# Moving one load four steps later, reshaping the warm-up and scaling rows a step sooner in a fused retention and feed-forward kernel

## The chip, the cores and the metric

The kernel runs on one core of a Trainium2 chip. The metric is device time in microseconds (us): the time of one execution, the median of the runs shown. The engines are named as in the profile: PE is TensorE's matmul stream and PEld its weight loads, DVE is VectorE, ACT is ScalarE, POOL is GpSimd, and SP is the engine whose queue issues nearly all the DMA transfers here. Each engine runs its own instructions strictly in the order in which they were built, and engines wait for one another only where one needs what another has made, or a buffer that another still uses.

## The reference

Per batch and head, scores between queries and keys are decayed by position and multiplied into the values; the result goes through a two-layer feed-forward block with the activation h - tanh(h).

```
ret = (scale * q @ k.T * Dmat) @ v        # 8 batches, 8 heads, 576 positions, 64 per head
x = ret laid out as (4608 tokens, 512)
h = x @ w_in                              # 512 -> 2048
out = (h - tanh(h)) @ w_out               # 2048 -> 512
```

## The kernel before, in words

The 576 positions are cut into 9 column chunks of 64, numbered c or n from 0 to 8; a chunk of all 8 batches gives 512 tokens. Within a chunk the retention part works on (chunk, batch) pairs numbered j = 8 c + b, as products inside the chunk plus a running state that carries what came before. The feed-forward part of chunk n runs over 16 slices f of the 2048 hidden values: `mm1(n, f)` makes a hidden slice (12 matmuls), `mm2(n, f)` multiplies it with a slice of w_out into four output banks o0 to o3 (12 matmuls). To keep precision each fp32 operand is split into two words, a high and a low one (names ending in h and l), and three products of words are added.

The work is staged in three parts.

1. **Seq part** (lines 583 to 629, `k` from 0 to 31): `mm1` of chunks 0 and 1, while the weights arrive and are split. Each weight slice passes through a chain over ACT and DVE (`guard` at lines 96 and 99, `unit` at lines 106 to 118, `finish` at line 125) that is advanced by `step()`. The hidden slices of chunks 0 and 1 are copied out of PSUM by ACT (lines 391 and 397) and spilled to DRAM, because w_out is not there yet. Retention work of chunks 0 and 1 is put in by `entry`. The keys of chunk 0 that build its states stand in two tiles, `krows[0]` and `krows[1]`; ACT multiplies each by a table (`scale_k`, line 576, four instructions each). `krows[1]` is loaded at k = 3 and scaled at k = 7, and first used at k = 8.
2. **Late part** (lines 630 to 642, 32 steps): `mm2` of chunk 1, steps 0 to 15, then of chunk 0, steps 16 to 31. Spilled slices are fetched back into three buffers (`fetch`, line 421, tiles named s), get their tanh and subtraction (`resume`, lines 426 and 427) and are split into words (`words`, lines 433 and 434). At step k the code issues, in this order: `words` of slice k + 1, `resume` of slice k + 2, `fetch` of slice k + 4, and the matmuls of slice k. At step 15 `mm2` closes chunk 1: its four banks are copied out by ACT and DVE (lines 468 and 470) and stored, and step 16 starts chunk 0 in the same banks.
3. **Main part** (lines 644 to 655): `mm1` and `mm2` of chunks 2 to 8 in turn, with retention of the next chunk put in between.

In the late and main parts retention is put in by `entry3(j)`, which computes the outputs of pairs j and j + 1 (and of j + 2, if b > 0), and at its end loads what the next one needs: the value rows (`vr`, `load_part(then, 1)`), a single column (`one`, `load_one`) and the queries and keys after that (`qk`, `load_part(.., 0)`). The first two parts of this data are needed early in the next `entry3`, the `qk` near its end, where it gives the next scores. `load_part(j, 0)` also loads the table of a new chunk (`qtab`, line 162), which stands in a single buffer. POOL multiplies each loaded tile by its table (`prep`, line 207). In the late part `entry3(16)`, `entry3(18)` and `entry3(21)` stand ahead of steps 3, 13 and 20.

All loads and stores of these parts are issued by SP, in order. An SP instruction that must wait (for a landed transfer or a buffer to come free) holds back all those behind it.

At the very start the PE runs warm-up matmuls on zeros (`busy`, line 498): 26 of 128 columns and 8 of 256 columns, ahead of the first scores, which wait for their data.

Of the kernel before, what the change touches and what calls it, by code (L numbers as in the profile page):

```python
# [19 lines left out]
P = 128  # L20
NF = DF // P
NCC = DM // P
C = 64
# [6 lines left out]


STEP = float(np.arctanh(0.5) / (1.06 * 2.0**-15))
WARM = 26

NI = NC * B

# [23 lines left out]
def behind(tc, name):  # L60

    tc.add_manual_dep(
        tc.nc.cur_bb.bb.instructions[-1], name,
        mybir.DependencyInfo(mybir.DependencyClass.Sync, mybir.DependencyReason.DATA), reason="paced",
    )
# [3 lines left out]
def retention_ffn(ctx: ExitStack, tc: tile.TileContext, ins, out, spill):  # L69
# [86 lines left out]
    def load_qtab(c):  # L156
        if c not in qtabs:
            if c == 1:
                qtabs[c] = const.tile([P, 4, C], F32, tag="wo6", name="qtab1")
            else:  # L160
                qtabs[c] = pool.tile([P, 4, C], F32, tag="qtab", bufs=1, name=f"qtab{c}")
            nc.sync.dma_start(qtabs[c], qtab_d[c - 1])

    def load_part(j, t):

        if j >= NI:
            return
        c, b = divmod(j, B)
        if t == 0:
            load_qtab(c)  # L170
        early = c == 1 and b // 2
        if early and early > 1:

            part = const.tile([P, 2, 2, 4, C], F32, tag=f"wo{2 * (early - 2) + t}", name=f"early{j}_{t}")
        elif early and t == 1:
            part = pool.tile([P, 2, 2, 4, C], F32, tag="one", bufs=1, name=f"vr{j}")
        else:
            part = pool.tile([P, 2, 2, 4, C], F32, tag=("qk", "vr")[t], bufs=2 - t, name=f"{('qk', 'vr')[t]}{j}")
        nc.sync.dma_start(part, qkv_d[c - 1, b : b + 2, :, 2 * t : 2 * t + 2].rearrange("u p t i s -> p u t i s"))
        if early and early > 1:  # L180
            behind(tc, pace[-1])
        parts[j, t] = part
        for u in range(2):
            loaded.setdefault(j + u, Parts([None, None])).parts[t] = part[:, u]
# [12 lines left out]
    def prep(j, t, n=2):  # L197

        if j >= NI:
            return  # L200
        c = j // B
        a = parts[j, t][:, :, 0]
        if t == 0:
            table = qtabs[c].unsqueeze(1).broadcast_to([P, n, 4, C])
        else:
            table = vtab[:, c].unsqueeze(1).unsqueeze(3).broadcast_to([P, n, 4, D])
        nc.gpsimd.tensor_tensor(a, a, table, op=ALU.mult)  # L207
# [16 lines left out]
    def m_score(j, sc):  # L224
        a = loaded[j]
        return [
            (sc[half(c), i], a[half(c), 1, i, :], a[half(c), 0, i, :], True, True) for i in range(4) for c in range(2)
        ]
# [23 lines left out]
    def run(same, other):  # L252

        while same or other:
            for ms in (same, other):
                for out_, w, x, start, stop in ms[:2]:
                    nc.tensor.matmul(out_, w, x, start=start, stop=stop)  # L257
                del ms[:2]

    def after_score(j, sc, n):  # L260

        if j < B:

            pm = pool.tile([P, 2, 4, C], F32, tag="gh", name=f"pm{j}")
            nc.vector.tensor_tensor(pm[:, 0], sc[:, 0], decay, op=ALU.mult)
        else:

            pm = parts[j, 0][:, :, 1]
            nc.vector.tensor_tensor(
                pm, sc, mask.unsqueeze(1).unsqueeze(1).broadcast_to([P, n, 4, C]), op=ALU.mult,  # L270
            )
        for u in range(n):
            scored[j + u] = pm[:, u]
# [20 lines left out]
    def bank(name, tag):  # L294
        return psp.tile([P, 2, 4, D], F32, tag=tag, bufs=2 if tag == "h" else 1, name=name)
# [5 lines left out]
    def pair(what, j, bank):  # L301
        return what(j, bank[:, 0]) + what(j + 1, bank[:, 1])
# [10 lines left out]
            more[1]()  # L313
        add_state(j, new)

    def entry3(j):


        c0, b = divmod(j, B)
        single, states = b > 0, c0 < NC - 1  # L320
        then = j + 2 + single
        o = bank(f"own{j}", "own")
        outs, scores = pair(m_out, j, o), []
        if single:
            two = bank(f"two{j + 2}", "new")
            run(m_score(j + 2, two[:, 1]), outs[:8])
            after_score(j + 2, two[:, 1:], 1)
            outs = outs[8:]
            if states:

                new = bank(f"new{j + 2}", "h")
                run(m_state(j + 2, new[:, 0]), outs[:8])
                outs = outs[8:]
                kept = pool.tile([P, 1, 4, D], F32, tag="cv", bufs=4, name=f"kept{j + 2}")
                nc.scalar.copy(kept, new[:, :1])
        if states:
            new = bank(f"new{j}", "h")
            run(pair(m_state, j, new), outs[:16])
            outs = outs[16:]
        if single:  # L340
            if not states:
                run([], outs)
            outs = m_out(j + 2, two[:, 0], True)
            if states:
                add_state(j, new)
            low = after_out(j, o, 2, False)
        if then < NI:
            sc = bank(f"s{then}", "h")
            scores = pair(m_score, then, sc)
        run(scores, outs)  # L350
        if not single:
            if states:
                add_state(j, new)
            low = after_out(j, o, 2, False)
        low()
        if then < NI:
            after_score(then, sc, 2)
        if single:
            if states:
                add_state(j + 2, kept, 1)  # L360
            after_out(j + 2, two[:, :1], 1)

        more = then % B > 0
        if then < NI:
            load_part(then, 1)
            prep(then, 1)
            if more:
                load_one(then + 2)
                prep(then + 2, 1, 1)
                prep(then + 2, 0, 1)  # L370
            load_part(then + 2 + more, 0)
            prep(then + 2 + more, 0)


    gs, ops, homes, obs = {}, {}, {}, {}
# [120 lines left out]
    def busy(n, cols):  # L496
        for _ in range(n):
            nc.tensor.matmul(wps[:, :cols], warm[:, :P], warm[:, :cols], start=True, stop=True)

    busy(WARM, P)  # L500
    busy(8, BLK // 2)
    decay = const.tile([P, 4, C], F32, tag="wo7", name="decay")
    krows = [const.tile([P, 4, 4, D], F32, tag=f"wo{4 + t}", name=f"krows{t}") for t in range(2)]
# [83 lines left out]
    first = 2 * B  # L587
    for k, (n, f) in enumerate(seq):
        last_two = k - (len(seq) - 2)
        if k in (2, 7):  # L590
            scale_k(k // 4)
        if k + 1 in early:
            scale_v(2 * early[k + 1])
        if last_two < 0:
            step()
        else:
            fetch(*late[2 + last_two])
        mm1(n, f, ("h", "o2", "h", "o3")[k % 4] if k < len(seq) - 4 else ("o2", "o3", "h", "h")[k % 4])
        if last_two < 0:
            step()  # L600
            if k < 24:
                step()
        if k in scales:
            scale_q(2 * scales[k])
        upto("load", k + (7 if k < 11 else 6))
        if k in (2, 5):
            load_pair(B + 4 + 2 * (k - 2) // 3)
        if k in (9, 10):
            load_part(first, k - 9)
        for f in [f for f in home if home[f] == (7, 13, 12, 11, 10)[k - NF]] if NF <= k < NF + 5 else []:  # L610
            nc.sync.dma_start(spill[0, f], homes[home[f]][:, (f + 1) % 2 if f > 1 else f])
        if k == 3:
            nc.sync.dma_start(krows[1], krows_d[1])
            behind(tc, pace[-1])
            sc = scores_of(3)
            ms, done = first_states(0, "new")
            run(pair(m_score, B, sc) + ms, [])
            after_score(B, sc, 2)
            done()
        if k in early:  # L620
            p = early[k]
            more = first_states(2 * (p - 3), f"o{(p + 1) % 2}") if p < B - 1 else None
            entry(2 * p, scores_of(p), more)
        if k == 14:
            load_part(first + 2, 0)
        if k == 26:
            prep(first, 1)
        if k == 28:
            prep(first + 2, 0)
    for k, (n, f) in enumerate(late):  # L630
        if k in (3, 13, 20):
            entry3(first + (0, 2, 5)[(3, 13, 20).index(k)])
        if 0 < k < len(late) - 1:
            words(*late[k + 1])
        if k < len(late) - 2:
            resume(*late[k + 2])
        if k + 4 < len(late):
            fetch(*late[k + 4])
        for _ in range(2 if k < 4 else 1):
            step()  # L640
        if k < len(late) - 1:
            mm2(n, f)
# [70 lines left out]
```

## Time and profile before

| | |
|---|---|
| time, median of 3 runs | 894.35 us (893.67 to 894.58) |
| time of the profiled execution | 894.74 us |
| span of the profiled execution, first to last instruction | 893.0 us |
| PE busy in the span | 874.8 us (98%) |
| DVE, ACT, POOL busy | 368.8 us, 293.5 us, 70.3 us |
| mean granted TensorE clock | 0.996 |

The span is what the trace covers; the 1.7 us between it and the time of that execution lie around it. Busy PE time counts the overlapped tails of pipelined matmuls, so a busy share of 98% says only that the stream is seldom empty. In rows of groups and timelines "x12" counts instructions, and what stands in brackets or behind "<-" is the wait just ahead of them and what ended it. A queue's own issue is written SPq, and its duration is that of issuing, not of the transfer. In the windows view each engine has its busy us and, in brackets, its instructions in that stretch; PEclk is the granted clock.

### The profile page before, as it was taken

The numbers are of one execution on the slowest core, as the hardware profiler recorded it, in microseconds if no ns is written. First come the engines' busy times: TensorE is split into PE (matmuls) and PEld (weight loads), VectorE is DVE, ScalarE is ACT, GpSimd is POOL, SyncE is SP. The second block draws the span as 40 slices with busy tenths as digits, with TensorE's granted clock in tenths as the row PEclk, the third lists the DMA queues.
The fourth block names the chain that finished last, engine by engine and source line by source line (L and its number), as shares of the span: only waits on it lengthen the run. The fifth ranks groups of instructions, "written<-read, shape, count | busy, mean of one in ns | idle before, by whom it ended". The sixth has DMA issues, their size and how long they took to land.

```text
span 893.0 us, 17735 instructions
## 1 busy us (share of the span) xinstructions
PE 874.8 (98%) x7848; PEld 723.6 (81%) x7848; DVE 368.8 (41%) x568; ACT 293.5 (33%) x522; POOL 70.3 (8%) x73
## 2 busy tenths in 40 slices
PE   7999999799999999999999999999999999999998
PEld 6777887588888888888888888888888888888886
DVE  6889876455333233323332334233332423223222
ACT  4787764334222222222222222222222322222222
POOL 0001002200011011101110101101110111000000
PEclk9999999999999999999999999999999999999999
DMA  9966955452212032202320131103220321002001
GB/s 346 360 201 217 345 169 166 136 160 78 60 61 77 1 95 72 79 1 64 103 69 10 49 111 44 43 6 90 72 78 1 93 73 49 1 1 47 1 1 47
DMA packets 37725, 82.06 MB, mean 92 GB/s; under 512 B 4241, under 2 KB 5393, under 8 KB 37649
## 3 DMA queue, kind: packets, MB, share of 16 engines
q1 hardware_dynamic: 37120, 80.02, 28.2%
q8 instruction: 61, 1.00, 0.5%
q10 hardware_dynamic: 528, 0.92, 0.3%
q14 instruction: 16, 0.12, 0.0%
HBM read 63.62 MB, written 17.30 MB: 91 GB/s over the span
## 4 chain that ended last, share of the span: by engine, by line
PE 85%; DMA 5%; DVE 4%; ACT 3%; issue 1%; POOL 0%; SPq 0%; DVEq 0%; POOLq 0%; ACTq 0%
PE o L451 42%; PE h L385 36%; DMA rwo<-in_w_out_dram 2%; PE new L257 2%; PE s L257 2%; PE own L257 1%; PE two L257 1%; DMA rwi<-in_w_in_dram 1%; DMA s<-spill_dram 1%; DVE mo L111 0%; DMA vr<-in_qkv_dram 0%; DVE mo L113 0%; DVE s L427 0%; DVE mo L106 0%; DMA spill_dram<-g 0%
## 5 line engine op out<-in xcount | busy, mean ns | idle before, releaser
L385 PE MATMUL h<-xh,wi 128*128 128x512 f32 x1152 | 302.4, 390 | 2.9 <-issue 1.1
L451 PE MATMUL o<-wo,gh 128*128 128x512 f32 x1144 | 292.3, 394 | 6.3 <-ACT ob L468 6.0
L451 PEld LDWEIGHTS o<-wo,gh 128*128 128x128 f32 x1144 | 213.9, 189 | 53.1 <-ACT ob L468 6.5
L385 PEld LDWEIGHTS h<-xh,wi 128*128 128x128 f32 x1152 | 215.3, 188 | 49.6 <-ACT wi L118 1.6
L412 DVE TENSOR_TENSOR g<-h,g 128x512 f32<-128x512 f32 x114 | 78.8, 691 | 341.4 <-ACT g L411 341.3
L411 ACT ACTIVATE g<-h 128x512 f32<-128x512 f32 x114 | 68.2, 598 | 364.2 <-PE h L385 362.5
L451 PE MATMUL o<-wo,gl 128*128 128x512 f32 x572 | 157.6, 390 | 0.0
L385 PE MATMUL h<-xl,wi 128*128 128x512 f32 x576 | 154.1, 389 | 0.0
L385 PEld LDWEIGHTS h<-xl,wi 128*128 128x128 f32 x576 | 108.1, 188 | 22.7
L451 PEld LDWEIGHTS o<-wo,gl 128*128 128x128 f32 x572 | 107.7, 188 | 22.6
L414 DVE TENSOR_TENSOR gl<-g,gh 128x512 fp32r<-128x512 f32 x113 | 81.4, 720 | 77.6 <-ACT gh L413 75.5
L413 ACT CAST gh<-g 128x512 fp32r<-128x512 f32 x113 | 70.1, 621 | 85.7 <-DVE g L412 85.7
L207 POOL TENSOR_TENSOR vr<-vr,vtab 128x512 f32<-128x512 f32 x21 | 23.1, 1100 | 626.9 <-DMA vr<-in_qkv_dram 540.9
L257 PE MATMUL own<-qk,state 64*64 64x64 f32 x736 | 45.2, 221 | 0.0
L257 PE MATMUL own<-qk,vr 64*64 64x64 f32 x736 | 44.1, 218 | 0.0
L257 PEld LDWEIGHTS own<-qk,vr 64*64 64x64 f32 x736 | 36.8, 135 | 0.0
L257 PEld LDWEIGHTS own<-qk,state 64*64 64x64 f32 x736 | 36.7, 134 | 0.0
L434 DVE TENSOR_TENSOR gl<-s,gh 128x512 fp32r<-128x512 f32 x30 | 22.7, 757 | 25.4 <-PE o L451 13.5
L207 POOL TENSOR_TENSOR qk<-qk,qtab 128x512 f32<-128x512 f32 x20 | 27.7, 1385 | 46.7 <-DMA qk<-in_qkv_dram 46.7
L433 ACT CAST gh<-s 128x512 fp32r<-128x512 f32 x30 | 18.6, 621 | 33.2 <-PE o L451 20.3
L427 DVE TENSOR_TENSOR s<-s,th 128x512 f32<-128x512 f32 x30 | 22.7, 757 | 8.1 <-ACT th L426 8.1
L257 PE MATMUL s<-qk 64*64 64x64 f32 x736 | 25.5, 219 | 0.0
(82 smaller groups left out, 560.6 us busy)
## 6 DMA issues: line engine op xcount, KB each, us to landing
qk<-in_qkv_dram SPq DMA_DIRECT2D x23, 512.0 KB, 5.8
vr<-in_qkv_dram SPq DMA_DIRECT2D x23, 512.0 KB, 4.4
out_dram<-ob SPq DMA_DIRECT2D x69, 128.0 KB, 2.4
rwi<-in_w_in_dram SPq DMA_DIRECT2D x16, 512.0 KB, 5.7
rwo<-in_w_out_dram SPq DMA_DIRECT2D x16, 512.0 KB, 5.3
s<-spill_dram SPq DMA_DIRECT2D x30, 256.0 KB, 2.7
one<-in_qkv_dram SPq DMA_DIRECT2D x14, 512.0 KB, 5.1
spill_dram<-g SPq DMA_DIRECT2D x20, 256.0 KB, 4.5
```

The costliest lines, as they stand in the source:

```text
L207: nc.gpsimd.tensor_tensor(a, a, table, op=ALU.mult)
L257: nc.tensor.matmul(out_, w, x, start=start, stop=stop)
L385: nc.tensor.matmul(hp, win[f][:, a, cc, :], x[:, cc, :], start=(k == 0), stop=(k == 3 * NCC - 1))
L411: nc.scalar.activation(g, h, AF.Tanh)
L412: nc.vector.tensor_tensor(g, h, g, op=ALU.subtract)
L413: nc.scalar.copy(gh, g)
L414: nc.vector.tensor_tensor(gl, g, gh.bitcast(F32), op=ALU.subtract)
L427: nc.vector.tensor_tensor(g, g, th, op=ALU.subtract)
L433: nc.scalar.copy(gh, g)
L434: nc.vector.tensor_tensor(gl, g, gh.bitcast(F32), op=ALU.subtract)
L451: nc.tensor.matmul(ops[n][t], g[:, t * P : (t + 1) * P], wout[f_][:, a, :], start=(f_ == first and k == 0), stop=(f_ == final and k == 2),)
```

## The change

The change has three edits.

First, in the late part `entry3` no longer loads the last piece, the `qk` (with a new chunk's `qtab`, and POOL's multiplication of the `qk`), at its end. It leaves the number in a list, and the loop does that load four steps later, at the head of steps 7, 17 and 25. The third `entry3` of the late part stands ahead of step 21, where it stood ahead of step 20. In the main part nothing moves.

Second, `WARM` matmuls of 192 columns are run, 18 of them, where 26 of 128 columns were. The 8 of 256 columns stay.

Third, `scale_k(1)` is called ahead of k = 6 of the seq part, where it was called ahead of k = 7.

```
-WARM = 26
+WARM = 18
...
-            load_part(then + 2 + more, 0)
-            prep(then + 2 + more, 0)
+            if later is None:
+                load_part(then + 2 + more, 0)
+                prep(then + 2 + more, 0)
+            else:
+                later.append(then + 2 + more)
...
-    busy(WARM, P)
+    busy(WARM, P + C)
...
-        if k in (2, 7):
+        if k in (2, 6):
             scale_k(k // 4)
...
+    rest = []
     for k, (n, f) in enumerate(late):
-        if k in (3, 13, 20):
-            entry3(first + (0, 2, 5)[(3, 13, 20).index(k)])
+        if k in (3, 13, 21):
+            entry3(first + (0, 2, 5)[(3, 13, 21).index(k)], rest)
+        if k - 4 in (3, 13, 21):
+            load_part(rest[0], 0)
+            prep(rest.pop(), 0)
```

On the SP queue, from the loads behind `entry3(18)` on, this stood before (s0_1 is the spilled slice f = 1 of chunk 0, which step 13 fetches; ob1 are the outputs of chunk 1 stored at step 15; vr21, one23 and qk24 are loads for the pairs of these numbers, qtab3 the table of chunk 3):

```order
L179 DMA vr21_2084<-in_qkv_dram 128x2x512
L193 DMA one23_2087<-in_qkv_dram 128x1024
L162 DMA qtab3_2091<-in_qtab_dram 128x256
L179 DMA qk24_2093<-in_qkv_dram 128x2x512
L421 DMA s0_1_2103<-spill_dram 128x512
L421 DMA s0_2_2124<-spill_dram 128x512
L421 DMA s0_3_2145<-spill_dram 128x512
L472 DMA out_0_dram<-ob1_2150 64x512 x8
L421 DMA s0_4_2179<-spill_dram 128x512
L421 DMA s0_5_2204<-spill_dram 128x512
```

The same stretch of the SP queue in the changed kernel:

```order
L179 DMA vr21_2076<-in_qkv_dram 128x2x512
L193 DMA one23_2079<-in_qkv_dram 128x1024
L425 DMA s0_1_2090<-spill_dram 128x512
L425 DMA s0_2_2111<-spill_dram 128x512
L425 DMA s0_3_2132<-spill_dram 128x512
L476 DMA out_0_dram<-ob1_2137 64x512 x8
L425 DMA s0_4_2166<-spill_dram 128x512
L162 DMA qtab3_2184<-in_qtab_dram 128x256
L179 DMA qk24_2186<-in_qkv_dram 128x2x512
L425 DMA s0_5_2196<-spill_dram 128x512
```

The fetches of s0_1 to s0_4 and the eight stores now stand ahead of the table and the qk24 load, not behind them.

On ACT, at k = 6 and 7 of the seq part, before (home is where the hidden slices h_6 and h_7 are copied to, mi and wi are weight slices in the making, vr a tile of value rows):

```order
L292 COPY state<-new_first_568 128x512
L391 COPY home_674<-h_6_661 128x512
L96 ACTIVATE mi_676<-rwi_466 128x512
L99 ACTIVATE mi_676<-mi_676 128x512
L118 CAST wi_681<-mi_555 128x512
L576 ACTIVATE krows_106<-krows_106,vtab 128x4x64 x4
L217 ACTIVATE vr_271<-vr_271,vtab 128x2x64 x4
L391 COPY home_674<-h_7_695 128x512
```

And in the changed kernel:

```order
L292 COPY state<-new_first_560 128x512
L580 ACTIVATE krows_98<-krows_98,vtab 128x4x64 x4
L395 COPY home_670<-h_6_657 128x512
L96 ACTIVATE mi_672<-rwi_458 128x512
L99 ACTIVATE mi_672<-mi_672 128x512
L118 CAST wi_677<-mi_547 128x512
L217 ACTIVATE vr_263<-vr_263,vtab 128x2x64 x4
L395 COPY home_670<-h_7_687 128x512
```

The four scaling instructions now stand ahead of the copy of h_6 and no longer between the weight chain and the scaling of vr.

More of the change, by code (lines that the diff above doesn't have):

```diff
@@ L314, in entry, with entry3 @@
         add_state(j, new)
-    def entry3(j):
+    def entry3(j, later=None):
         c0, b = divmod(j, B)
```

## The prediction

> **What bounds the kernel now.** I read the page first, then who waited for whom on PE, then the stretches where PE waited.
>
> ```profile
> span 893.0 us, 17735 instructions
> ...
> PE 874.8 (98%) x7848; PEld 723.6 (81%) x7848; DVE 368.8 (41%) x568; ACT 293.5 (33%) x522; POOL 70.3 (8%) x73
> ...
> q8 instruction: 61, 1.00, 0.5%
> ```
>
> PE is the bound: the others are busy for less than half of the span. Time can only come from PE's gaps. PE's waits over the whole span, with total, times and longest:
>
> ```profile
> PE o L451 <- ACT ob L468: 6.0, 1, 6.0
> PE s_first L257 <- DMA a<-in_first_dram: 2.5, 4, 1.3
> ...
> PE h L385 <- issue: 1.1, 1, 1.1
> ...
> PE s L257 <- ACT wi L118: 0.8, 1, 0.8
> PE h L385 <- ACT wi L118: 0.6, 1, 0.6
> PE o L451 <- ACT gh L433: 0.2, 1, 0.2
> ```
>
> One wait of 6.0 us stands out. The timeline around it, all engines (start, us, engine, line, operation):
>
> ```profile
> 169.90 0.73 POOL L207 TENSOR_TENSOR one<-one,qtab 128x256 f32<-128x256 f32 x1
> ...
> 170.66 0.33 SPq L162 DMA_DIRECT2D qtab<-in_qtab_dram  x1
> ...
> 171.04 0.43 SPq L179 DMA_DIRECT2D qk<-in_qkv_dram  x1
> ...
> 171.56 1.36 SPq L421 DMA_DIRECT2D s<-spill_dram  x3
> 171.65 0.39 PE L451 MATMUL o<-wo,gl 128*128 128x512 f32 x1
> ...
> 176.92 0.63 ACT L426 ACTIVATE th<-s 128x512 f32<-128x512 f32 x1 [6.75 <-DMA s<-spill_dram]
> 177.46 1.05 ACT L468 COPY ob<-o 128x512 f32<-128x512 f32 x2
> ...
> 178.08 4.21 PE L451 MATMUL o<-wo,gh 128*128 128x512 f32 x8 [6.04 <-ACT ob L468]
> ```
>
> Read it backwards. PE at step 16 wants the bank o0, which ACT must copy out first. ACT's copies stand behind the tanh of s0_1, which waited 6.75 us for its fetch. SP issued that fetch only at 171.56, because the table load at 170.66 waited until POOL had finished with the old table (the "one" product of 169.90), and SP is in order. Three fetches then left at once, behind the qk load. The stall has a tail, seen in windows (first PE's busy us and instructions, then PEld's and the others'; behind them the granted clock):
>
> ```profile
> 175.82:178.08 2.26, 0.00 (x1) 0.00 (x1) 0.50 (x1) 1.16 (x3) 1.27 (x1) 0.50 0.42 160
> 178.08:182.65 4.57, 4.51 (x10) 3.23 (x11) 2.59 (x5) 1.81 (x4) 0.00 (x0) 0.50 0.50 117
> ...
> 185.40:190.00 4.60, 4.60 (x22) 3.82 (x21) 2.04 (x4) 2.33 (x4) 0.00 (x0) 1.00 0.59 179
> ```
>
> After the idle stretch the clock is granted at half, until 182.65: 10 matmuls in 4.57 us, where 22 take 4.60 us at full clock.
>
> **The change part by part.** First the moved load. The price of the stall: from the matmul at 171.65 to the next at 178.08 are 6.43 us, where a step of 12 takes 2.72 us (the chain of waits, below), so 0.23 each: 6.2 us lost. The 10 slow matmuls take 4.57 us for 2.27 us: 2.3 us more. Together 8.5 us. With the fetch of s0_1 ahead of the table, SP issues it when its buffer comes free, not at 171.56. What it costs then is bounded by these rows, the chain at the like place behind `entry3(16)` and the page's times to landing:
>
> ```profile
> 136.65 4.79 DMA s<-spill_dram
> 141.46 0.64 ACT th L426
> ...
> 144.06 16.64 PE o L451 x72
> ...
> 227.46 2.72 PE o L451 x12
> ...
> qk<-in_qkv_dram SPq DMA_DIRECT2D x23, 512.0 KB, 5.8
> vr<-in_qkv_dram SPq DMA_DIRECT2D x23, 512.0 KB, 4.4
> ...
> s<-spill_dram SPq DMA_DIRECT2D x30, 256.0 KB, 2.7
> ...
> one<-in_qkv_dram SPq DMA_DIRECT2D x14, 512.0 KB, 5.1
> ```
>
> At step 3 the fetch left behind vr, one and qk, took 4.79 us to its tanh, and PE lost only the 0.2 us of the last wait row. In the changed kernel one 512 KB load fewer stands ahead of it, so that 0.2 us goes, and at step 13 the same fetch takes between 2.7 (undisturbed) and 4.8 us. With two loads ahead I put it at 3 to 4 us, in time for its tanh two steps on (5.4 us, less what ACT's own work takes) or up to half a microsecond late. Chunk 0 then starts in banks that DVE and ACT copy out while PE finishes chunk 1; the last bank is copied after its last matmul, and the copy is needed 3 matmuls (0.7 us) into step 16, so a little may be lost there. I take 0.3 us new stall, with 0 and 2 as bounds.
>
> What the move itself may cost: the table and qk24 now follow the fetch of s0_4 at step 16, about 174.5 if step 16 starts at 171.9 (171.65 plus one matmul). POOL was done with the old table at 170.6, so SP does not stop there. qk lands 5.8 us later and POOL needs 1.3 more: about 181.6. The scores that read it come near the end of the third `entry3`, now ahead of step 21, at 171.9 + 5 x 2.72 = 185.5 and later: 4 us of cover. One `entry3` a step later only changes the order of work. In each moved place the next fetch leaves behind a qk load and has two steps (5.4 us) until its tanh; the row of 4.79 says that this holds, and what it costs if not: 0.2 us each, three times.
>
> Second, the scaling a step sooner. ACT's timeline, PE's at the same place, and the tile's load:
>
> ```profile
> 43.45 0.59 ACT L391 COPY home<-h 128x512 f32<-128x512 f32 x1 [3.60 <-PE h L385]
> ...
> 45.68 1.71 ACT L576 ACTIVATE krows<-krows,vtab 128x256 f32<-128x256 f32 x4
> 47.29 1.27 ACT L217 ACTIVATE vr<-vr,vtab 128x128 f32<-128x128 f32 x4
> ...
> 42.79 1.55 PE L385 MATMUL h<-xh,wi 128*128 128x512 f32 x6 [1.08 <-issue]
> ...
> L613 SPq DMA_DIRECT2D krows<-in_krows_dram x1: 1261/1261/1261, 31.4 to 31.4; - x1
> ...
> DMA to landing us min/median/max: 10.1/10.1/10.1
> ```
>
> PE in the two later stretches of the seq part where it waits (length, PE busy):
>
> ```profile
> 56.00:58.70 2.70, 1.88 (x11) 1.00 0.53 170
> ...
> 69.60:70.70 1.10, 0.50 (x4) 1.00 0.78 309
> ```
>
> The load lands at 31.4 + 10.1 = 41.5. ACT stands idle for 3.6 us until 43.45, so the four scalings fit in from 41.5 to 43.1, and the 1.6 us that they held back the vr scaling (45.68 to 47.29) go from ACT's chain. What PE gets of that is the 0.8 us wait between 56 and 58.7; the 0.6 us near 70 I leave standing, since a faster PE only helps there if ACT, which by then works on what PE has just made, is faster too. If the load lands later than 41.8, ACT loses what it is later by.
>
> Third, the warm-up. Its rows, by start, time and count, and PE's wait for the second scores:
>
> ```profile
> 2.01 0.85 PE L498 MATMUL wps<-warm 128*128 128x128 bf16 x6
> ...
> 4.15 0.85 PE L498 MATMUL wps<-warm 128*128 128x256 bf16 x3
> ...
> 5.50 0.27 PE L257 MATMUL s_first<-a 64*64 64x64 f32 x2
> ...
> 6.83 0.45 PE L257 MATMUL s_first<-a 64*64 64x64 f32 x8 [0.64 <-DMA a<-in_first_dram]
> ```
>
> A 128-column one starts every 0.107 us and a 256-column one every 0.213, so 192 columns take 0.16: 18 make 2.88 us where 26 made 2.78. The first scores come 0.1 us later, and 0.64 us of waiting for data at 6.83 covers that: nothing. The second effect is that every PE instruction behind it stands 16 places earlier in the stream (8 weight loads, 8 matmuls). Instructions are fetched by DMA while the kernel runs, 61 packets of 16 KB on q8, and 15,696 of the 17,735 are PE's (7848 matmuls and as many loads); the 1.08 us wait "issue" at 42.79, inside a run of matmuls that wait for nobody, looks like such a fetch that came late, in a stretch that is full of other DMA. [...] From rows alone: with the wait kept, PE gains the 0.8 us, up to 1.1 with the small slips before it; with the wait gone, PE is 1.1 us early but soon meets the weight chain, and the two together are at most the ACT gain of 1.6. I take 1.2 us between 0 and 1.6; 0 if the loads of w_out, which the later stretch waits for, give nothing back.
>
> The sum: -8.5 (stall and slow clock) - 0.2 (step 7) + 0.3 (new stall) - 1.2 (seq part) = -9.6 us. Against the profiled 894.74 that is 885.1; the median was 0.39 lower, so 884.8.
>
> [...]
>
> **The rivals.** *A remnant of the stall.* The fetch of s0_1 lands 2 to 4 us late behind vr21 and one23, or the out stores hold SP, and ACT's copies still wait. For it: the 4.79 row, and ACT's order is unchanged. Against it: at step 3 three loads were ahead and 0.2 us was lost. It gives back 2.4 to 6 us: 887.2 to 891.
>
> *The wait is not SP's.* If the banks are late for another reason than the tanh ahead of the copies, only the seq part gains: about 893.2. Against it: ACT waited 6.75 us for that very fetch.
>
> *More late instruction fetches.* All 61 block boundaries move by 16 instructions, and the place of each against the fast 64 x 64 stages of `entry` and `entry3` is new. Each late fetch costs the 1.1 us of the "issue" row. From 11 new ones on (9.6 + 1.8 over 1.1) the kernel is slower than before by over 0.2%; with 12 it is 898. Against it: one boundary in 61 showed it before, and the main part has little DMA.
>
> **How the numbers follow.** 0.2% of 894.35 is 1.8 us, about what a measurement of this kernel can tell. The forecast has 0.80: from 883.0 (894.35 - 8.7, no new stall, 1.6 from the seq part, the 0.6 us near 70 gone too, and half of the 0.9 us by which the runs differ) to 887.2 (894.35 - 8.7 + 1.0 of new stall + 0.6 for the moved loads, nothing from the seq part). The remnant has 0.12, the wrong cause 0.05, the fetches 0.03. The range takes in the near part of the remnant: 883.0 to 888.5. Faster is the forecast and nearly all of the remnant, 0.92; within 0.2% are cases near 893, 0.05; slower 0.03.
>
> **What would show it.** Right: no PE wait over 1 us after 60 us, the granted clock at 1.00 from 170 to 190, the s fetch at step 13 issued near 166, ACT's krows rows near 41.5 and PE's 0.8 us wait gone. The "issue" row gone or moved tells on the fetch. Wrong: PE waiting for ob copies again, a half clock, PE waiting for qk in the third `entry3`, ACT waiting for krows beyond 43.4, or several "issue" rows.

## The result, and the profile after

The changed kernel takes 885.25 us, the median of 4 runs (884.32 to 885.74); the kernel before took 894.47 us beside it (893.67 to 895.04, 4 runs). The ratio is 0.9896, with a 95% interval from 0.9879 to 0.9913: faster by some 9.2 us, inside the range. The lines behind the edit of `entry3` have moved by four: L451, L468 and L385 of before are L455, L472 and L389 here.

The profiled execution took 885.74 us; the head of its page:

```profile
span 884.0 us, 17719 instructions
...
PE 874.5 (99%) x7840; PEld 725.0 (82%) x7840; DVE 367.3 (42%) x568; ACT 293.6 (33%) x522; POOL 70.0 (8%) x73
...
q8 instruction: 61, 1.00, 0.5%
```

PE was busy for nearly as long as before (874.8 us). Of the 9.0 us that went from the span 8.7 are gaps; a busy PE at half clock counts as busy in both. PE's waits, the whole list (total, times, longest):

```profile
PE own_first L257 <- issue: 1.6, 1, 1.6
PE wps L502 <- DVE warm L496: 1.2, 1, 1.2
PE s_first L257 <- DMA a<-in_first_dram: 1.0, 2, 0.8
PE h L389 <- ACT wi L118: 0.6, 1, 0.6
PE h L389 <- ACT xh L283: 0.5, 1, 0.5
```

The 6.0 us for ob, the 0.8 us for wi, the 0.2 us for gh and the "issue" wait in the h matmuls are gone. The 0.6 us near 70 is still there. New is an "issue" wait of 1.6 us at the very start, which nothing in the forecast had.

The place of the old stall, from the timelines of SP, POOL and ACT, in order of time:

```profile
164.87 5.23 SPq L425 DMA_DIRECT2D s<-spill_dram  x3
...
168.46 0.73 POOL L207 TENSOR_TENSOR one<-one,qtab 128x256 f32<-128x256 f32 x1
168.64 0.63 ACT L430 ACTIVATE th<-s 128x512 f32<-128x512 f32 x1
169.17 0.57 ACT L472 COPY ob<-o 128x512 f32<-128x512 f32 x1
170.26 0.59 ACT L472 COPY ob<-o 128x512 f32<-128x512 f32 x1 [0.52 <-PE o L455]
...
175.98 0.54 SPq L425 DMA_DIRECT2D s<-spill_dram  x1
176.61 0.39 SPq L162 DMA_DIRECT2D qtab<-in_qtab_dram  x1
177.06 0.43 SPq L179 DMA_DIRECT2D qk<-in_qkv_dram  x1
```

The fetch of s0_1 leaves at 164.87, before POOL is done with the old table and not behind it. It takes 3.28 us to land (before, 5.34). Its tanh at 168.64 has no wait in its row, where it had 6.75 us. The two bank copies follow at once, and now ACT waits for PE (0.52), not PE for ACT. The table's load at 176.61 finds the old table free for seven microseconds.

The scaled rows, in ACT's timeline:

```profile
41.95 1.71 ACT L580 ACTIVATE krows<-krows,vtab 128x256 f32<-128x256 f32 x4
44.41 0.59 ACT L395 COPY home<-h 128x512 f32<-128x512 f32 x1 [0.75 <-PE h L389]
...
46.66 1.27 ACT L217 ACTIVATE vr<-vr,vtab 128x128 f32<-128x128 f32 x4
```

They stand at 41.95, ahead of the copy of h_6, and ACT still waits 0.75 us for PE behind them: here they cost nothing. In the changed kernel run once more (e11 below), where PE came to h_6 two microseconds sooner, ACT waits 0.98 us for their load and the copy follows them without a wait, so there the cover is used up.

The windows (PE's busy us and instructions first, the granted clock third from the end) show the clock at the start and at the place of the old stall:

```profile
11.68:15.09 3.41, 1.77 (x65) 1.44 (x64) 2.34 (x7) 1.23 (x3) 0.00 (x0) 1.00 1.03 402
15.09:18.50 3.41, 2.94 (x34) 2.62 (x35) 2.98 (x7) 3.15 (x7) 0.00 (x0) 0.50 1.03 392
18.50:21.92 3.42, 3.42 (x9) 2.67 (x8) 3.27 (x6) 0.83 (x2) 0.00 (x0) 0.50 1.05 378
...
165.00:175.00 10.00, 10.00 (x45) 7.77 (x44) 7.22 (x11) 5.57 (x10) 2.71 (x3) 1.00 0.64 194
175.00:190.00 15.00, 14.87 (x244) 12.42 (x243) 7.72 (x14) 6.04 (x11) 1.29 (x1) 1.00 0.61 175
```

From 165 to 190 PE is busy for 24.87 of 25.00 us, at full clock. But from 15.09 to 21.92, 6.83 us, the clock is granted at half, where the kernel before kept 1.00 (15.39 to 22.22).

Where the 9.0 us came from, by the starts of PE's first matmul of each slice in the two traces, and, for later, in the trace of the changed kernel run once more (e11 below):

| stretch of PE's work | before | changed | changed again |
|---|---|---|---|
| start to h_6 | 39.15 | 41.35 | 39.37 |
| h_6 to late step 0 | 83.08 | 80.43 | 80.62 |
| steps 0 to 7 | 24.70 | 24.01 | 24.01 |
| steps 8 to 14 | 22.23 | 22.23 | 22.23 |
| step 15 | 8.92 | 2.72 | 2.72 |
| step 16 | 5.20 | 3.12 | 3.12 |
| steps 17 to 23 | 22.26 | 22.67 | 23.27 |
| step 24 to the end | 687.41 | 687.43 | 687.53 |

The late part gave 8.6 us (2.08 at step 16, 6.20 at step 15, 0.69 ahead, less 0.41 behind). The seq part gave 2.65 behind h_6 and lost 2.20 ahead of it.

### The profile page after: what moved, and what is told of

It reads as the page before. It is cut to its first block, busy times and chain, and to the rows that moved or that the text cites. A ratio compares the mean times of both kernels' runs of the same rounds, so it can differ in the third digit from the quotient of the medians.

```text
span 884.0 us, 17719 instructions
## 1 busy us (share of the span) xinstructions
PE 874.5 (99%) x7840; PEld 725.0 (82%) x7840; DVE 367.3 (42%) x568; ACT 293.6 (33%) x522; POOL 70.0 (8%) x73
## 4 chain that ended last, share of the span: by engine, by line
PE 97%; DMA 1%; DVE 1%; ACT 0%; issue 0%; SPq 0%; DVEq 0%
PE o L455 45%; PE h L389 44%; PE new L257 2%; PE s L257 2%; PE own L257 2%; PE two L257 1%; DMA a<-in_first_dram 1%; PE new_first L257 0%; PE s_first L257 0%; PE own_first L257 0%; DVE mi L111 0%; ACT mi L99 0%; PE wps L502 0%; SPq L511 0%; ACT xh L283 0%
## 5 line engine op out<-in xcount | busy, mean ns | idle before, releaser
L389 PE MATMUL h<-xh,wi 128*128 128x512 f32 x1152 | 303.4, 392 | 1.1 <-ACT wi L118 0.6
L455 PE MATMUL o<-wo,gh 128*128 128x512 f32 x1144 | 290.2, 392 | 0.0
L389 PEld LDWEIGHTS h<-xh,wi 128*128 128x128 f32 x1152 | 216.5, 189 | 47.1 <-ACT wi L118 1.4
L455 PEld LDWEIGHTS o<-wo,gh 128*128 128x128 f32 x1144 | 212.9, 188 | 45.6 <-DVE ob L474 0.7
L455 PE MATMUL o<-wo,gl 128*128 128x512 f32 x572 | 157.3, 389 | 0.0
L389 PE MATMUL h<-xl,wi 128*128 128x512 f32 x576 | 154.4, 390 | 0.0
L389 PEld LDWEIGHTS h<-xl,wi 128*128 128x128 f32 x576 | 108.5, 188 | 22.8
L455 PEld LDWEIGHTS o<-wo,gl 128*128 128x128 f32 x572 | 107.3, 188 | 22.4
L207 POOL TENSOR_TENSOR vr<-vr,vtab 128x512 f32<-128x512 f32 x21 | 22.7, 1079 | 598.3 <-DMA vr<-in_qkv_dram 481.9
L257 PE MATMUL own<-qk,state 64*64 64x64 f32 x736 | 45.2, 221 | 0.0
L257 PE MATMUL own<-qk,vr 64*64 64x64 f32 x736 | 44.1, 218 | 0.0
L257 PEld LDWEIGHTS own<-qk,vr 64*64 64x64 f32 x736 | 36.8, 135 | 0.0
L257 PEld LDWEIGHTS own<-qk,state 64*64 64x64 f32 x736 | 36.7, 134 | 0.0
L207 POOL TENSOR_TENSOR qk<-qk,qtab 128x512 f32<-128x512 f32 x20 | 27.5, 1377 | 69.1 <-DMA qk<-in_qkv_dram 63.9
L257 PE MATMUL s<-qk 64*64 64x64 f32 x736 | 25.8, 219 | 0.0
L257 PEld LDWEIGHTS s<-qk 64*64 64x64 f32 x736 | 23.4, 135 | 1.4 <-issue 1.1
```

The source lines that it names most:

```text
L389: nc.tensor.matmul(hp, win[f][:, a, cc, :], x[:, cc, :], start=(k == 0), stop=(k == 3 * NCC - 1))
L455: nc.tensor.matmul(ops[n][t], g[:, t * P : (t + 1) * P], wout[f_][:, a, :], start=(f_ == first and k == 0), stop=(f_ == final and k == 2),)
```

## The experiments

Times are medians with the lowest and highest run; the kernel before took 894.5, 894.6, 894.9 and 894.8 us beside the four groups. Diffs are against the kernel that each names. The theory, as in the prediction: SP's queue held by the table's load made the stall; "issue" waits are instruction blocks fetched late; the rows scaled early free PE's 0.8 us. Rivals are named in each expectation.

### One edit at a time

**e1, the moved load alone**, against the changed kernel:

```
-WARM = 18
+WARM = 26
-    busy(WARM, P + C)
+    busy(WARM, P)
-        if k in (2, 6):
+        if k in (2, 7):
```

> Only the moved load, and the third entry3 one step later; warm-up and scaling as before. Theory A (the stall at step 16 and its slow clock were SP held by the table load, and nothing takes their place): 8.5 us of stall and slow clock and 0.4 us at step 7 go, so 894.5 - 8.9 = 885.6 us, with the start up to 143 us as in the kernel before, its wait 'issue' near 42 included. Theory B (part of the gain of the changed kernel came from the seq part, as predicted): about 886.5, since 1.2 us are then missing from it.

885.96 us (885.80 to 886.88, 4 runs), ratio 0.9908 (0.9894 to 0.9921): 8.5 us from this edit alone, where the forecast's terms for it make 8.4 (8.5 and 0.2, less 0.3). The two values expected lie 0.9 us apart with the median between them, so the time does not choose between them. What is left among PE's waits:

```profile
PE h L389 <- issue: 1.6, 2, 1.0
...
PE s L257 <- ACT wi L118: 0.8, 1, 0.8
PE o L455 <- DVE ob L474: 0.2, 1, 0.2
```

In the trace the 0.8 us that belongs to the scaling and the "issue" waits stand, and the new wait at the bank copies is 0.2 us (step 16 is 0.62 longer than a step of 2.72).

**e2, the warm-up alone**, against the kernel before:

```
-WARM = 26
+WARM = 18
-    busy(WARM, P)
+    busy(WARM, P + C)
```

> Only the warm-up: 18 of 192 columns where 26 of 128 were. Theory A (the edit moves the boundaries of the instruction stream: the late fetch near 42 goes, but one near 12.5 comes, inside the first outputs, and PE's emptiness there can bring two windows of half clock): 1.2 us gained at 42, 2.2 us lost before 22, so +1.0: 895.4 us, with a wait 'issue' of 1 to 2 us between 11 and 15 and none near 42. Theory B (the wait near 12.5 in the changed kernel was chance): 894.1 us, 0.4 us gained by the fetch near 42, no wait near 12.5.

895.22 us (893.00 to 897.49, 11 runs), ratio 1.0008 (0.9996 to 1.0019): not told from no change, and the two values expected lie too close together for this spread. The trace says more than the time:

```profile
PE own_first L257 <- issue: 1.2, 1, 1.2
...
PE s L257 <- ACT wi L118: 0.8, 1, 0.8
```

The "issue" wait in h is gone and one in own_first has come. h_6 to late step 0 takes 81.95 us for 83.08, and the start 0.45 us more. The execution of the trace took 893.22 us and kept its clock until the old stall. Of the eleven runs seven have a mean granted clock of 0.992 or less, and these take 894.87 to 897.49 us; of the 21 runs of the kernel before beside it one has.

**e3, the scaling alone**, against the kernel before:

```
-        if k in (2, 7):
+        if k in (2, 6):
             scale_k(k // 4)
```

> Only the scaling of the second krows tile a step sooner. Both theories: the four scalings run in ACT's idle time while PE's fetch wait near 42 lasts, the vr scaling starts 1.6 us sooner, and PE's waits between 56 and 58.7 (0.8 us and a little) go: 1.1 us gained, 893.4 us, the stall at step 16 as before.

893.43 us (891.63 to 896.22, 11 runs), ratio 0.9991 (0.9982 to 1.0001): the expected time, though the interval just takes in no change. The trace has the wi wait of 0.8 gone, and h_6 to late step 0 is 81.35 us, 1.73 less. Further on it gives some back, since PE comes sooner and the fetches of the late part do not keep up:

```profile
PE o L451 <- ACT ob L468: 4.8, 1, 4.8
...
PE o L451 <- ACT gh L433: 1.3, 1, 1.3
```

The gh wait at step 7 grows from 0.2 to 1.3 us: that stall too was SP's order, and a PE that is earlier runs deeper into it. In the whole change the moved load has taken it away.

**e4, load and scaling without the warm-up edit**, against the changed kernel:

```
-WARM = 18
+WARM = 26
-    busy(WARM, P + C)
+    busy(WARM, P)
```

> The changed kernel without its warm-up edit. Theory A: the start as before (no late fetch near 12.5, the one near 42 there), so 1.1 us better than the load alone: 884.4 us, 0.8 us faster than the changed kernel. Theory B (the start of the changed kernel was chance): the same as the changed kernel, or 0.4 us slower, 885.3 to 885.7 us.

886.69 us (883.62 to 887.50, 5 runs), ratio 0.9899 (0.9881 to 0.9916). The median lies above both values expected. The idea that the loss at the start needs the new warm-up falls here: with the old warm-up the trace has the same wait and the same half clock, at the same place:

```profile
10.47:13.88 3.41, 1.77 (x68) 1.22 (x57) 3.05 (x8) 1.36 (x3) 0.00 (x0) 1.00 0.99 320
13.88:17.29 3.41, 2.69 (x64) 2.53 (x65) 1.64 (x5) 1.18 (x3) 0.00 (x0) 0.50 0.99 370
17.29:20.70 3.41, 2.95 (x21) 2.37 (x19) 3.01 (x7) 2.45 (x6) 0.00 (x0) 0.50 0.96 327
```

Its five runs fall into two groups, 883.62 and 884.21 at a mean granted clock of 0.999 and 1.000, and 886.69 to 887.50 at 0.995 and 0.996. The loss is one that an execution has or has not. Whether the new warm-up makes it more frequent stays open; e2's clocks speak for it.

### What held the fetch: the table, or the loads ahead

**e7, the table four steps later, the queries and keys at their old place**, against e1:

```
-    def load_part(j, t):
+    def load_part(j, t, table=True):
...
-        if t == 0:
+        if t == 0 and table:
...
+                load_part(then + 2 + more, 0, False)
                 later.append(then + 2 + more)
...
-            load_part(rest[0], 0)
+            load_qtab(rest[0] // B)
```

> The kernel before with the late load split: the queries and keys (qk24, 512 KB) are loaded where they were, ahead of the fetch of s0_1; only the table (qtab3) and POOL's product come four steps later. Theory A (the stall came from SP standing still until POOL was done with the old table): s0_1 is issued some 5 us sooner, as in the kernel with the whole load moved (885.96), and lands at most 1 us later than there for one 512 KB load more ahead of it: 885.6 to 887.0, longest late PE wait under 1.2 us. Rival B (the number of loads ahead of the fetch is what counts): a stall of 2 us or more at step 16 remains, with its half clock: 888.5 or more.

887.87 us (887.12 to 889.76, 6 runs), ratio 0.9917 (0.9900 to 0.9935). That is between the two: over theory A's 887.0, under rival B's 888.5. The timelines of SP, ACT and PE say which part is which:

```profile
164.53 0.43 SPq L179 DMA_DIRECT2D qk<-in_qkv_dram  x1
165.68 5.35 SPq L425 DMA_DIRECT2D s<-spill_dram  x3
...
171.39 0.63 ACT L430 ACTIVATE th<-s 128x512 f32<-128x512 f32 x1 [1.54 <-DMA s<-spill_dram]
171.92 1.05 ACT L472 COPY ob<-o 128x512 f32<-128x512 f32 x2
...
172.54 0.50 PE L455 MATMUL o<-wo,gh 128*128 128x512 f32 x1 [0.83 <-ACT ob L472]
```

SP stands still no longer: the fetch leaves at 165.68, 0.25 us from where it leaves in e1 (165.43). But it leaves behind 512 KB more, and its tanh waits 1.54 us, so the banks come 0.83 us late. The clock stays full. The fetch takes 5.68 us to land, for 3.31 in e1. Of the 8.5 us the table's wait was some 6.7 (894.6 less 887.9). The rest, 1.8 to 1.9 us, goes with the load ahead: steps 15 and 16 take 3.72 and 3.64 us here and 2.72 and 3.34 in e1, and step 19 takes 0.6 more, where PE waits for a slice whose fetch left at 179.10 (176.85 in e1), behind the later stores. A is right on the main cause and had the second too small.

**e8, the load one step later instead of four**, against e1:

```
-        if k - 4 in (3, 13, 21):
+        if k - 1 in (3, 13, 21):
```

> The kernel before with the same load one step later instead of four: the table's load then stands behind the fetch of s0_1 (step 13) and ahead of that of s0_2 (step 14), and the table is still held by POOL until about 170.6. Theory A (SP's standstill only moves on to s0_2): s0_2 leaves near 171.5 behind qk24 and lands near 176 to 177; its tanh is due one step (2.7 us) after that of s0_1, so PE loses 1 to 2 us near steps 17 and 18: about 887 to 888.5, and a late PE wait on gl, gh or ob of over 0.8 us. Rival B (it is enough that s0_1 stands ahead of the table): as with four steps, 885.5 to 886.5, no late wait over 0.5 us.

888.17 us (887.07 to 890.23, 6 runs), ratio 0.9922 (0.9902 to 0.9942), as theory A has it. SP, ACT and PE:

```profile
165.96 0.33 SPq L425 DMA_DIRECT2D s<-spill_dram  x1
170.61 0.33 SPq L162 DMA_DIRECT2D qtab<-in_qtab_dram  x1
...
171.51 0.89 SPq L425 DMA_DIRECT2D s<-spill_dram  x2
...
176.78 0.63 ACT L430 ACTIVATE th<-s 128x512 f32<-128x512 f32 x1 [4.33 <-DMA s<-spill_dram]
...
178.90 2.12 PE L455 MATMUL o<-wo,gh 128*128 128x512 f32 x8 [0.82 <-ACT gh L437]
```

SP's standstill, from 166.3 to 170.6, has moved one fetch on: s0_2 now leaves at 171.51, its tanh waits 4.33 us, and PE waits 0.82 at step 17. Steps 6 and 7, where the first moved load now stands one step on, are 0.68 too long for a like reason. The price is smaller than before the change because only PE's next words, not the bank copies, stand behind that tanh. A load four steps on is past the table's last use.

### The "issue" waits

**e6, 26 warm-up matmuls of another shape**, against the changed kernel:

```
-    busy(WARM, P + C)
+    busy(8, C)
+    busy(WARM, P + C // 2)
```

> The changed kernel with its warm-up as 8 matmuls of 64 and 18 of 160 columns: 26 instructions again, as before the change, and about the same time (8 x 0.053 + 18 x 0.133 = 2.8 us). Theory A (the wait named issue near 42 us hangs on how many instructions stand ahead of it, since a block of instructions ends there): it returns, 1.2 to 1.5 us inside h_7's matmuls as in the four profiles with 26 warm-ups (1.47, 1.36, 1.24, 1.34), time about 886 to 887. Rival B (it hangs on the length of the warm-up matmuls or on chance): no wait over 0.3 us near 42, as in the two profiles with 18. The wait inside own_first near 13 us is expected by A to be seldom over 1 us with 26 (1 of 4 profiles), by B as after the change (1.2 to 1.6).

885.07 us, one run. The wait is back, at the same matmul, but smaller than theory A had it, and the time is below A's 886 to 887:

```profile
PE own_first L257 <- issue: 0.8, 1, 0.8
...
PE h L389 <- issue: 0.4, 1, 0.4
```

PE came there at 41.96 instead of 41.33 and went on at 42.74 instead of 42.79: the end did not follow PE over these 0.6 us, so the wait is as long as PE is early.

**e9, 34 warm-up matmuls of 96 columns, and e12, the same kernel timed**, against the changed kernel:

```
-WARM = 18
+WARM = 34
-    busy(WARM, P + C)
+    busy(WARM, 96)
```

> The changed kernel with 34 warm-up matmuls of 96 columns (34 x 0.08 = 2.7 us): 16 PE instructions more than before the change, so that a block's end falls 8 matmuls earlier in the work. Theory A (late fetch of a block of instructions): the wait named issue near 42 us falls 8 matmuls earlier, into h_6 or early h_7, and grows by up to 8 x 0.23 = 1.8 us, to 2 to 3.2 us, since the fetch comes no sooner. Rival B: no wait there, or again 1.2 to 1.5 us in the same place.

> The changed kernel with 34 warm-up matmuls of 96 columns, timed now (one run gave 888.88, with waits named issue of 2.86 and 1.50 us in h_6 and h_8 to h_14's stretch). Theory A: both waits return in its profile at the same matmuls (601st and 984th), and the time is 2 to 4.5 us above the changed kernel of this call: 887.3 to 889.7. Rival B (the single run was chance): within 1 us of the changed kernel.

e9: 888.88 us, one run, with PE's row `PE h L389 <- issue: 4.4, 2, 2.9`. e12: 889.16 us (886.98 to 889.59, 6 runs), ratio 0.9930 (0.9911 to 0.9949), 4.1 us above the changed kernel of the same group. Same work, same warm-up time to 0.2 us, only 32 PE instructions more. e12's waits and windows:

```profile
PE h L389 <- issue: 3.4, 2, 2.3
```

```profile
38.82:42.23 3.41, 1.23 (x22) 0.91 (x19) 2.84 (x6) 2.88 (x7) 0.00 (x0) 1.00 1.02 401
42.23:45.64 3.41, 3.30 (x8) 2.59 (x8) 1.00 (x2) 0.00 (x0) 0.00 (x0) 0.50 0.81 305
```

Theory A holds: with the block's end 8 matmuls earlier in the work, PE's stop there (from one matmul's start to the next) is 2.69 us in e12 and 3.26 in e9, where it was 1.47 before. The whole difference stands in this part: h_6 to late step 0 takes 84.95 us in e12 and 80.62 in e11. A second late block shows, and behind the 3.41 us in which PE was busy for 1.23 come 3.41 us at half clock.

**e10, 10 warm-up matmuls of 320 columns, and e11, the changed kernel once more**, e10 against the changed kernel:

```
-WARM = 18
+WARM = 10
-    busy(WARM, P + C)
+    busy(WARM, 320)
```

> The changed kernel with 10 warm-up matmuls of 320 columns (10 x 0.27 = 2.7 us, as long as before): 16 PE instructions fewer than in the changed kernel. In all profiles so far a block of instructions ends at the 221st to 222nd matmul of the stream and another at the 601st to 602nd, whatever the warm-up. Theory A (block ends at fixed counts): the wait inside own_first now falls 8 small matmuls later, which is only some 0.3 us of work, so it stays at up to 1.5 us when the fetch is late; near 42 no wait, the end falls 16 matmuls behind where the kernel before has it (3.6 us of cover). Time as the changed kernel within 0.7 us: 884.5 to 886. Rival B (fewer PE instructions ahead is better throughout): no own_first wait, 883 to 884.

> The changed kernel once more, as the yardstick for the two others of this call: 884.3 to 886.0, median near 885.2, no wait named issue near 42. If the half clock near 15 to 22 us depends on how late the fetch inside own_first comes, it is there when that wait is over 1.5 us and not when it is shorter; it costs about 2 us, so that single runs should fall into two groups near 883.5 and 885.5.

e10: 885.20 us (883.77 to 887.05, 5 runs), ratio 0.9889 (0.9868 to 0.9911). e11: 885.03 us (884.65 to 888.38, 6 runs), ratio 0.9896 (0.9873 to 0.9918). No wait in h near 42 in either, as theory A has it. In e10 no "issue" wait stands in own_first, as B has it, but PE waits 1.4 us for data there, h_6 begins at 39.35 as in e11 (39.37), and the time is the same, so B's gain falls. The wait in own_first that A expected does not show either; the wait for data may cover it. e11's wait in own_first was 0.8 us and its clock stayed full, its profiled run is at 884.65; that its six runs fall into two groups was not borne out (five lie from 884.65 to 885.33, one at 888.38).

What the traces of all these kernels show together, counting PE's matmuls from the start of the stream: the wait in h comes at the 601st or 602nd matmul whenever there is one, with 26 and with 34 warm-ups. That in own_first comes at the 221st or 222nd, with 18 and with 26. The second one in e1, e9 and e12 comes at the 984th or 985th, with 26 and with 34. And each of them ends 1.3 to 1.6 us after a packet on q8 has ended (41.28 and 42.79 before, 12.98 and 14.25 in the changed kernel, 41.02 and 42.34 in e12). So these waits belong to a count in the instruction stream and not to the work that stands there. The distances of 380 and 383 matmuls, with as many weight loads, are 760 and 766 instructions; how many instructions a block holds, and why just these block ends were late, no run shows.

### What the moved load costs where it now stands

**e14, the load behind the step's fetch**, against the changed kernel:

```
-        if k - 4 in (3, 13, 21):
-            load_part(rest[0], 0)
-            prep(rest.pop(), 0)
...
             fetch(*late[k + 4])
+        if k - 4 in (3, 13, 21):
+            load_part(rest[0], 0)
+            prep(rest.pop(), 0)
```

> The changed kernel with the moved load issued behind the step's fetch instead of ahead of it (at steps 7, 17 and 25), nothing else. Step 20 took 6.22 and 6.80 us in the two profiles of the changed kernel, where 5.77 is its length without a wait; the tanh of slice 21 there waits 2.5 to 2.7 us for its fetch, which leaves behind the table and qk24. Theory A (those 0.4 to 1.0 us are the price of the two loads ahead of that fetch): step 20 takes 5.77 to 5.9 us, the tanh's wait shrinks by at least 1 us, and the time is 884.2 to 885.0, 0 to 0.9 below the changed kernel (885.0 to 885.3). Rival B (the fetch is late because the eight stores held SP until 176, or the loads just hit the next fetch instead): step 20 stays at 6.1 or more, or step 21 loses as much; 885 to 886.

884.33 us (883.80 to 884.42, 4 runs), ratio 0.9885 (0.9867 to 0.9903). In the changed kernel ACT's tanh of slice 21 (the slice that PE takes at step 21, s0_5) had waited for a fetch that left behind the table and qk24:

```profile
183.38 0.63 ACT L430 ACTIVATE th<-s 128x512 f32<-128x512 f32 x1 [2.48 <-DMA s<-spill_dram]
```

In e14 (SP, then ACT's tanhs of slices 20 and 21):

```profile
173.99 1.03 SPq L425 DMA_DIRECT2D s<-spill_dram  x2
175.11 0.38 SPq L162 DMA_DIRECT2D qtab<-in_qtab_dram  x1
...
176.83 0.63 ACT L430 ACTIVATE th<-s 128x512 f32<-128x512 f32 x1 [1.79 <-DMA s<-spill_dram]
...
178.80 0.63 ACT L430 ACTIVATE th<-s 128x512 f32<-128x512 f32 x1
```

Slice 21 waits no longer: its fetch lands after 3.17 us, where it took 5.78 and 6.01 in the changed kernel's two traces, and step 20 takes 5.77 us where it took 6.22 and 6.80, as theory A has it. But eight traces hold the load ahead of that fetch (the changed kernel's two, e1, e4, e6, e9, e10 and e12), and only four of them pay for it. Where the fetch took 5.37 to 6.01 us to land (the changed kernel's two, e4 and e6), step 20 is 0.40 to 1.03 us too long; where it took 4.90 to 5.28, it is 5.77. This is the fastest kernel of the study by its median, 0.7 to 0.9 us under the changed one. Its interval overlaps that of the changed kernel, so that it is faster is not shown; that the late fetch is gone is.

## Why the prediction was right, and where it was not

The total was 0.45 us off: 884.8 against 885.25. By its own steps:

- **The stall, -6.2**: step 15 went from 8.92 to 2.72 us, 6.20. The cause was split by e7 and e8: mostly the table's wait on SP, as said, and some 1.9 us the 512 KB ahead of the fetch, which the forecast had left inside the same sum. The fetch of s0_1 took 3.28 us to land, within the 3 to 4 of the forecast.
- **The slow clock, -2.3, and the new stall, +0.3**: together -2.0, and step 16 went from 5.20 to 3.12, -2.08. It is 0.40 above a step of 2.72 in the changed kernel, 0.40 to 0.98 in the others without a stall, within the bounds of 0 and 2. Its whole loss before was 5.20 less 2.72, 2.48 us.
- **Step 7, -0.2**: steps 4 to 7 gave 0.67. This term was mis-sized: the row of 0.2 names one wait of the stretch, and steps 4, 5 and 7 each ran 0.05 to 0.16 us long beside it, which only the lengths of the steps show.
- **The moved loads, 0, at worst 0.6**: 0.41 in the profiled execution and 1.01 in e11, all at step 20. What failed is that "the row of 4.79 says that this holds": the fetch of slice 21 left behind the table and qk24 and took 5.78 and 6.01 us, more than its two steps of 5.4, and cost more than 0.2. The late tanh pushes its subtraction on DVE up to the mask product of the third `entry3`, and PE waits for that (0.5 us among e11's waits, PE L257 for DVE L269). e14 takes it away. The third `entry3` one step later, which no run tries alone, shows no cost: steps 17 to 23 take 22.26 us before and 22.23 in e1.
- **The seq part, -1.2, "the two together are at most the ACT gain of 1.6"**: this bound failed. Behind h_6 the warm-up gave 1.1 (e2) and the scaling 1.7 (e3), and both together gave 2.65. They nearly add, because PE does not meet the weight chain again: with the 0.8 us wait gone, no wait for wi is left until the 0.6 us near 70, which stayed as forecast. That the "issue" wait in h goes when 8 matmuls fewer stand ahead of it, no run had shown before; e2, e14 and both traces of the changed kernel have none there. The 8 matmuls follow from the count of instructions ahead alone (16 fewer, half of them weight loads).
- **The start, 0**: the profiled execution lost 2.20 us there. This was nowhere in the forecast. It took back more than the 1.45 us that the seq part gave beyond the forecast, and that is why the total fits so well: two misses, of -1.45 and +2.20, of opposite sign. The closeness of the total is luck; the stall, its clock and its cause are not. In e11, without the half clock, the span is 882.9 us, 10.1 under before, and the changed kernel's part in the start is 0.2 us.

Of the rivals, the remnant of the stall is what e8 shows (0.82 us at step 17), but four steps are enough to be clear of it. That the wait is not SP's is excluded by e1, e7 and e8. The late fetches were given 0.03 and a price of 1.1 us each from eleven on; e12 shows that the price was too low. Two of them cost 4.1 us with the half clock that the longer one brings. That the stops go by the count is shown (the 221st, 601st and 984th matmul or the next, whatever the warm-up): what a change in the count does depends on which of the 61 block ends are late, and the trace before does not tell that.

What stays open: why the block that ends at the 221st matmul comes at 10.8 to 11.3 us in some executions and at 12.3 to 13.1 in others. All five traces with 18 or 10 warm-ups have it late, and four of the nine with 26 or 34, so the warm-up may bear on it, which these few do not settle. It shares the DMA with bulk loads (share 0.98 to 1.04 in these windows), but no run here changed those. Nor was a kernel with two tables run, in which the table's load need not wait for the last use of the old one.

## What to carry to other kernels

When an engine waits for a transfer, look at when it was issued and what its queue was doing then: here SP stood 6.1 us at the table's load, until POOL was done with the old table (SPq L162 for POOL L207 in the trace before), and the fetch of s0_1 behind it left only at 171.56. The load that stops is the one to move. Move it past the last use of its buffer (e1, four steps on: 885.96 us), not by the least that reorders the queue (e8, one step on: 888.17), and put it behind the fetch that is due next (3.17 us to landing there, 4.90 to 6.01 behind the load). And a change in the count of PE's instructions, even in a warm-up, moved the places in the work at which PE stopped for an instruction block: 32 more cost 4.1 us with the same work (e12), which must be set apart before such a change is credited or blamed.

## What the runs showed that was not expected

- The stops for instruction blocks come at the same matmuls of the stream whatever the warm-up: after the 221st with 18 and 26 warm-ups, after the 602nd with 26 and 34, after the 985th with 26 and 34 (in some traces one earlier). Each ends 1.3 to 1.6 us after its packet on q8. The packet follows PE's earlier course: in e4, where PE was some 2 us late from the start, it ended at 43.51 and the stop at 44.92, for 41.28 and 42.79 before.
- The half clock came behind stretches in which PE was not idle throughout. It lasts 3.41 us in e12 (42.23 to 45.64) and 6.83 in the changed kernel (15.09 to 21.92); in the 3.41 us ahead of it PE was busy for 1.23 in e12, and for 1.77 in the changed kernel and in e4. Behind 3.41 us with 2.07 busy (before, 11.98 to 15.39) the clock stayed at 1.00, but so it did behind 1.76 in e12 (11.51 to 14.92) and 1.77 in e1 (4.06 to 7.47). So busy time as this profile counts it does not tell which stop costs the clock. e14's stop in own_first, 1.5 us by its "issue" row, cost none: the clock there is 1.00 from 6.32 to 43.87 us.
